# Attention backward: the crossbar transposes that TensorE still did, and GpSimd copies for dK, dV and dQ

## The chip, the cores and the metric

The kernel runs on one core of one Trainium2 chip. The core has five engines that each work through their own list of instructions in order: TensorE (PE in the profile, with its weight loads as PEld), VectorE (DVE), ScalarE (ACT), GpSimd (POOL) and SyncE (SP). SP computes nothing here; it issues DMAs, among them DMAs that transpose 128x128 blocks of two-byte elements on their way (DMA_TRANSPOSE, "the crossbar" below). POOL issues DMAs too. The metric is the device time of one execution in microseconds, as the median of several runs.

## The reference

The reference is one transformer block with adaptive layer norm, and the gradient of its output for nine of its inputs. With S = 2048 tokens, D = 512 and H = 32 heads of 16 columns each:

```
x = x + ga * (softmax(q k^T * 16**-0.5) v) wo        q, k, v = (layernorm(x)*(1+ca)+sa) wqkv
x = x + gb * (relu(h w1 + b1)**2 w2 + b2)            h = layernorm(x)*(1+cb)+sb
```

The change lies in the backward pass of the attention. For each head it forms again P = exp(scores), then dP = dO V^T (with the softmax correction folded into two extra columns), dS = P * dP, and from these

```
dV = P^T dO      dK = dS^T Q      dQ = dS K
```

dV and dK contract over queries, dQ over keys, so that dQ needs dS with its two axes turned.

## The kernel before, in words

The program has three stages: the forward pass with the weight gradients of the dense layer (to about 1166 us of the profiled span), the attention backward (`attn_bwd`, to about 2385 us), and a tail with the remaining weight gradients and the input gradient (`phase6`).

`attn_bwd` goes through 16 pairs of heads (g from 0 to 7, jp 0 or 1). A pair is worked off in 16 groups, numbered m: four chunks c of 512 keys, and in each the 16 blocks ib of 128 queries, four to a group. One query block against one chunk, for both heads, is a unit; i is its number in its group. For a unit

- TensorE makes the scores of each head (line 1608, `st`) and, a unit later, dP of each head (line 1522, `dp`); the two use different halves of the array's rows and run together;
- ACT takes the exponential (line 1611, `pu`);
- VectorE multiplies dS = dP * P (line 1526, `ds`). In ten of the 16 groups one of the eight products goes by ACT (a copy, line 1540) and POOL (line 1541) instead;
- TensorE adds to dK and dV of the chunk (line 1459, `acckv`). When all 16 query blocks of a chunk are in, ACT writes the sum to `kvT` (line 1462), still with features on partitions.

When a group's four units are done, `dS()` has SP issue one crossbar transpose of the group's 32 blocks of dS (line 1549, `dsT<-ds`; one of five destinations is a piece of a larger tile and is named `keep`). In the first group of each chunk TensorE turns four of the 32 blocks instead (line 1565, against an identity matrix), ACT copies them out of PSUM (line 1566), and SP's DMA takes 28. Below, T(m) is the crossbar transpose of group m.

dQ of two groups (`dq`, line 1484, `accq`) is put into TensorE's list two groups after the second of them was transposed: eight calls, two in each even unit. TensorE works in order: where `dsT` has not landed when such a matmul comes up, all that stands behind it waits as well, the next `st` and `dp` first.

When a pair is complete, its results have to be turned once more, tokens onto partitions. Both halves of `kvT` (8 blocks each) and `dqT` (4 blocks, written by VectorE on line 1492) go into a list `turnq`, and at the fourth unit of a group of the next pair (from group 2 on for `kvT`, from 7 on for `dqT`) one entry is taken: TensorE turns its blocks (lines 1472, 1500) into a PSUM buffer of the same three that `st` uses, and ACT copies them, spread over the heads' columns, into `dk_t`, `dv_t`, `dq_t` (lines 1476, 1502).

POOL meanwhile issues the loads for the next pairs (line 1597), about one for each group, each behind a copy of one element (`tick`, line 1596) that ties the load to the progress of VectorE.

The order on every engine in this stage is the order of the program; nothing is rearranged by a scheduler that matters here.

Of the kernel before, what the change touches and what calls it, by code (L numbers as in the profile page):

```python
# [9 lines left out]
BF16 = mybir.dt.bfloat16  # L10
# [9 lines left out]
P = 128  # L20
DH = 16
# [84 lines left out]
class K:  # L106
# [1284 lines left out]
    def load_group(self, g):  # L1391
# [5 lines left out]
        if g < 2:  # L1397
            T, o = {}, 0
            for n, e in width.items():
                if g:  # L1400
                    T[n] = qp.tile([P, e], BF16, name=f"{n}g")[:]
                elif n == "K":
                    T[n] = self.keep[:, :e]
                else:
                    T[n] = self.q0[:, o:o + e]
                    o += e
            self.Tq[g] = T
        T, pieces = self.Tq[g % 2], []
        for n, (src, rows) in fm.items():
# [21 lines left out]
    def attn_bwd(self):  # L1431
# [7 lines left out]
        tc, nc = self.tc, self.nc  # L1439
        S, D, H, NQ, ST, SC = self.S, self.D, self.H, self.NQ, self.ST, self.SC  # L1440
        G = 4
        W = 4 * DH
        kvp, stp, dpp = self.kvp, self.stp, self.dpp
# [3 lines left out]
        nc.vector.memset(acckv[:], 0.0)  # L1447
        accq = accp.tile([P, 512], F32, name="accq")
        masked, kvs = self.masked, self.kvs
        pend, pendq, turnq, two = [], [], [], []  # L1450
        own = dT_free[-1]

        def kv(u):
            (T, g, jp, c, ib, kvT, pu, ds) = u
            for j, (n, src) in enumerate((("Q", ds), ("dO", pu))):
                for a in range(2):
                    r = 64 * j + 32 * a
                    col = (2 * jp + a) * DH
                    nc.tensor.matmul(acckv[r:r + DH, :], lhsT=T[n][:, ib, col:col + DH], rhs=src[:, a, :],  # L1459
                                     start=(ib == 0), stop=(ib == ST - 1))  # L1460
            if ib == ST - 1:
                nc.scalar.activation(kvT[:, 512 * c:512 * (c + 1)], acckv[:], ACT.Copy, scale=kvs[:])

        def turn(g, jp, kvT, s0):

            if kvT is None:
                return turn_q(g, jp)
            h0 = 4 * g + 2 * jp
            n = ST // 2
            tp = stp.tile([P, n, P], BF16, name="st")  # L1470
            for st in range(n):
                nc.tensor.transpose(tp[:, st, :], kvT[:, (s0 + st) * P:(s0 + st + 1) * P], self.ident[:])
            v = tp[:].rearrange("p s (t a e) -> p t s a e", t=2, a=2)
            for t, dst in enumerate((self.dk_t, self.dv_t)):
                d = dst[:, s0:s0 + n, h0 * DH:(h0 + 2) * DH].rearrange("p s (a d) -> p s a d", a=2)
                nc.scalar.copy(d, v[:, t, :, :, 0:DH])

        def dq(u):
# [12 lines left out]
            if (c, ib0) == (SC - 1, ST - 2 * G):  # L1491
                nc.vector.tensor_scalar(self.dqT[:], accq[:], self.scale, None, ALU.mult)
                turnq.append((g, jp, None, 0))

        def turn_q(g, jp):

            h0 = 4 * g + 2 * jp
            tp = stp.tile([P, ST // G, P], BF16, name="st")
            for b in range(ST // G):
                nc.tensor.transpose(tp[:, b, :], self.dqT[:, b * P:(b + 1) * P], self.ident[:])  # L1500
            for h in range(2):
                nc.scalar.copy(self.dq_t[:, 8 * h:8 * h + 8, h0 * DH:(h0 + 2) * DH].rearrange("p (s i) e -> p s i e", i=2),
                               tp[:, 2 * h:2 * h + 2, :].rearrange("p i (s e) -> p s i e", s=G))

        def kv_two(n=2):
            for _ in range(n):
                u = pend.pop(0)
                kv(u)
                (T, g, jp, c, ib, kvT, pu, ds) = u
                if ib < ST - 1:  # L1510
                    continue
                if c % 2 and (g, jp) == (NQ - 1, 1):
                    turnq.append((g, jp, kvT, 4 * (c - 1)))
                elif c == SC - 1:
                    turnq.extend((g, jp, kvT, s0) for s0 in (0, ST // 2))

        def dP(u, a):

# [9 lines left out]
        def odd(c, ib):  # L1528
            return (c * SC + ib // G) % 2 == 1

        def no_turn(c, ib):
            return ib // G > 0

        def off(c, ib):
            return odd(c, ib) or (c > 1 and ib // G == 2)
# [1 line left out]
        def dP_pool(u, dp):  # L1537
            (T, g, jp, c, ib, kvT, pu, dsg, i, grp) = u
            f = (self.junk6, self.csq)[(c * SC + ib // G) % 2]
            nc.scalar.copy(f[:], dp[:])  # L1540
            nc.gpsimd.tensor_tensor(dsg[:, i, 1], f[:], pu[:, 1, :], ALU.mult)  # L1541
# [26 lines left out]
        tick = self.tick  # L1568
        wmt = self.load_wmt()
        T = self.T0  # L1570
        last = None
        for g in range(NQ):
            for jp in range(2):
                if jp == 0:
                    if g + 1 < NQ:
                        Tn, later = self.load_group(g + 1)
                    else:
                        Tn, later = None, self.wq_pieces(1) + wmt[2 * g + 1:]
                    cut = len(later) // 2 if Tn else len(later)
                    pieces = self.pair_pieces(g, 1) + wmt[2 * g:2 * g + 1] + later[:cut]  # L1580
                    later = wmt[2 * g + 1:2 * g + 2] + later[cut:]
                elif g + 1 < NQ:
                    pieces = self.pair_pieces(g + 1, 0) + later
                else:
                    pieces = [(self.xhat1_6[:, st, :], self.xhat1_d.rearrange("(st p) d -> p st d", p=P)[:, st, :])
                              for st in range(ST)]
                kvT = kvp.tile([P, S], BF16, name="kvT")
                end = (g, jp) == (NQ - 1, 1)
                total = len(pieces)
                for c in range(SC):  # L1590
                    c0 = 512 * c
                    for ib0 in range(0, ST, G):
                        m = c * (ST // G) + ib0 // G
                        while pieces and ((total - len(pieces)) * SC * ST <= m * G * total or m == SC * ST // G - 1):
                            if last:
                                nc.gpsimd.tensor_copy(tick[:], last[7][0:1, 0, 0, 0:1])
                            nc.gpsimd.dma_start(*pieces.pop(0))
                        dsg, grp = self.dsp.tile([P, G, 2, 512], BF16, name="ds"), []
                        for i in range(G):
                            ib = ib0 + i  # L1600
                            q = slice(ib * P, (ib + 1) * P)
                            if turnq and i == 3 and m >= (7 if turnq[0][2] is None else 2):
                                turn(*turnq.pop(0))
                            pu = self.pup.tile([P, 2, 512], BF16, name="pu")
                            for a in range(2):
                                stt = stp.tile([P, 512], F32, name="st")
                                rs = slice(64 * jp, 64 * jp + 64)
                                nc.tensor.matmul(stt[:], lhsT=T["QT"][rs, q], rhs=masked["KT"][a][rs, c0:c0 + 512],  # L1608
                                                 start=True, stop=True)
                                held = dP(last, a) if last else None  # L1610
                                nc.scalar.activation(pu[:, a, :], stt[:], ACT.Exp, scale=self.scale)  # L1611
                                if held is not None:
                                    dP_pool(last, held)
                                if a == 0 and i % 2 == 1 and odd(c, ib) and len(pend) >= 4:
                                    kv_two(1)
                            if last:
                                dS(last)
                            last = (T, g, jp, c, ib, kvT, pu, dsg, i, grp)
                            if i % 2 == 1 and len(pend) >= 4:
                                kv_two(1 if odd(c, ib) else 2)  # L1620
                            elif i % 2 == 0 and len(pendq) > 2 * G:
                                for _ in range(4 if end else 2):
                                    dq(pendq.pop(0))
                            if i == 2:
                                turn_ds(dsg, grp, no_turn(c, ib), end and m > 2)
            T = Tn
        with tc.manual_schedule(engines=ALL):
# [23 lines left out]
            self.cs_bc(2)  # L1651
            turn(*turnq.pop(0))
            self.dw_mm(k1, 1, 1, 0, ST)
        assert not turnq and not pend
        self.dw_open = [(1, 0, k0), (2, 0, v0), (1, 1, k1)]

    def dw_mm(self, pt, t, kt, a, b):
# [308 lines left out]
```

## Time and profile before

| what | value |
|---|---|
| median of 3 runs | 2506.41 us (2501.06 to 2510.86) |
| span of the profiled execution, first to last instruction | 2498.5 us |
| what the median has beyond that span (2506.41 - 2498.5) | 7.9 us |
| attention backward in that span | about 1166 to 2385 us |
| granted TensorE clock, mean | 0.998 |
| PE, ACT, DVE, POOL busy, share of the whole span | 96%, 91%, 68%, 30% |
| DMA_TRANSPOSE from `ds` in the stage | 256: 208 to `dsT`, 48 to `keep` |

No separate total time is given for the profiled execution; its span is set against the runs by the difference in the third row.

How to read it: shares over the whole span mix three stages, so each stage is read by its own stretch. A row of a group has the line, the engine, the operation, the tiles (out<-in) and the count, then busy time and the mean of one, then the engine's idle time just before these instructions, and what ended it. SP's DMA instructions are not counted as busy anywhere, but the timeline of the SP queue has a start and a duration for each, where the duration is the time that the instruction held the queue, not the time to landing. A row of the timeline with x4 covers four instructions, from the start of the first to the end of the last.

### The profile page before, as it was taken

The page shows a single profiled execution, that of the slowest core. Times are in us where ns is not written, and L with a number is a line of the kernel's source. Part 1 is how long each engine was busy: PE and PEld are TensorE (multiplying, and loading weights), DVE is VectorE, ACT ScalarE, POOL GpSimd, SP SyncE. Part 2 cuts the span into 40 slices and gives each one's busy share as a digit, 9 for nine tenths or more (in the row PEclk, how much of TensorE's full clock was granted, in tenths as well). Part 3 has the DMA queues.
Part 4 walks back from the last instruction along what each step waited for, and adds up shares of the span by engine and source line. Part 5 has one row for each costly group of instructions (what it writes and reads, how often), then busy time and mean ns, then how long its engine had stood idle before and what let it go on. Part 6 is the DMA issues. An engine that isn't in the chain of part 4 may idle for free.

```text
span 2498.5 us, 67897 instructions
## 1 busy us (share of the span) xinstructions
PE 2410.2 (96%) x26211; PEld 1061.6 (42%) x26439; DVE 1695.0 (68%) x3487; ACT 2283.1 (91%) x3757; POOL 753.5 (30%) x1337
## 2 busy tenths in 40 slices
PE   8999999999999999999999999999999999999998
PEld 4555555555555555583233332333333333333343
DVE  6222322422332343576999999999999999999957
ACT  7999999999999997534999999999999999999945
POOL 2344531220131022245222323322333222322223
PEclk9999999999999999999999999999999999999999
DMA  4589661541243045499999999999999999999997
GB/s 166 135 179 208 169 125 47 132 100 40 92 114 98 23 123 147 110 199 216 232 235 233 232 227 231 237 234 231 230 235 239 234 230 236 234 233 236 238 217 192
DMA packets 1293547, 454.13 MB, mean 182 GB/s; under 512 B 1236948, under 2 KB 1261398, under 8 KB 1293222
## 3 DMA queue, kind: packets, MB, share of 16 engines
q1 hardware_dynamic: 1252422, 344.68, 71.8%
q0 software_dynamic: 38720, 104.04, 13.9%
q8 instruction: 207, 3.39, 0.6%
q10 hardware_dynamic: 2080, 1.05, 0.2%
q14 instruction: 118, 0.97, 0.1%
HBM read 75.83 MB, written 64.49 MB: 56 GB/s over the span
## 4 chain that ended last, share of the span: by engine, by line
PE 49%; ACT 35%; DMA 7%; issue 5%; DVE 3%; POOL 1%; SPq 1%; ACTq 0%; DVEq 0%; POOLq 0%
ACT pu L391 26%; PE st L1608 17%; PE acckv L1459 8%; ACT pu L1611 6%; DMA dsT<-ds 5%; PE accq L1484 5%; PE st L388 4%; PE dp L1522 2%; PE accbank L322 2%; PE dps L1050 2%; PE dp L1659 1%; PE st L1754 1%; ACT csq L1540 1%; PE pps L1237 1%; DVE ds L1526 1%
## 5 line engine op out<-in xcount | busy, mean ns | idle before, releaser
L1526 DVE TENSOR_TENSOR ds<-dp,pu 128x512 bf16<-128x512 f32 x1888 | 1166.0, 682 | 34.6 <-PE dp L1522 19.1
L1611 ACT ACTIVATE pu<-st 128x512 bf16<-128x512 f32 x2048 | 1073.8, 666 | 34.7 <-PE st L1608 21.3
L391 ACT ACTIVATE pu<-st 128x1024 bf16<-128x1024 f32 x992 | 912.1, 1077 | 4.2 <-PE st L388 3.7
L388 PE MATMUL st<-QTm,KTq 128*128 128x512 bf16 x1859 | 560.9, 377 | 27.1 <-ACT pu L391 6.1
L322 PEld LDWEIGHTS <-pu 128*128 128x128 bf16 x8192 | 346.7, 96 | 236.1 <-issue 3.0
L1522 PE MATMUL dp<-kvm,q 64*128 64x512 bf16 x1024 | 365.0, 384 | 2.0 <-DVE ds L1526 0.7
L322 PE MATMUL accbank<-Vaug,pu 128*128 128x17 bf16 x8192 | 357.4, 171 | 8.3 <-ACT Vaug L522 1.1
L1522 PE MATMUL dp<-kvm,dOTg 64*128 64x512 bf16 x1024 | 363.6, 383 | 0.3
L1608 PE MATMUL st<-kvm,q 64*128 64x512 bf16 x1024 | 349.4, 382 | 5.4 <-ACT pu L1611 0.2
L1608 PE MATMUL st<-kvm,QTg 64*128 64x512 bf16 x1024 | 348.1, 381 | 6.5
L1541 POOL TENSOR_TENSOR ds<-csq,pu 128x512 bf16<-128x512 f32 x128 | 147.2, 1150 | 627.0 <-ACT csq L1540 553.6
L388 PEld LDWEIGHTS <-KTq 128*128 128x128 bf16 x1984 | 188.4, 96 | 176.9 <-issue 124.8
L1459 PE MATMUL acckv<-ds,Qg 128*16 128x512 bf16 x1024 | 176.2, 382 | 0.3
L1459 PE MATMUL acckv<-pu,q 128*16 128x512 bf16 x1024 | 176.3, 383 | 0.0
L1459 PE MATMUL acckv<-ds,q 128*16 128x512 bf16 x1024 | 176.2, 383 | 0.0
L1459 PE MATMUL acckv<-pu,dOg 128*16 128x512 bf16 x1024 | 176.0, 382 | 0.0
L302 POOL DMA_DIRECT2D QTm<-QTq_d x124 | 63.1, 511 | 341.5 <-PE st L388 320.0
L1608 PEld LDWEIGHTS <-q 64*128 64x128 bf16 x1024 | 67.0, 94 | 163.5 <-issue 150.6
L1608 PEld LDWEIGHTS <-QTg 64*128 64x128 bf16 x1024 | 67.1, 94 | 160.6 <-issue 145.7
L329 DVE RECIPROCAL rl<-accbank 128x4 f32<-128x4 f32 x128 | 22.9, 179 | 158.3 <-PE accbank L322 158.2
L1522 PEld LDWEIGHTS <-q 64*128 64x128 bf16 x1024 | 88.8, 93 | 52.9 <-issue 43.3
L1522 PEld LDWEIGHTS <-dOTg 64*128 64x128 bf16 x1024 | 88.2, 93 | 52.9 <-issue 43.8
(390 smaller groups left out, 3055.1 us busy)
## 6 DMA issues: line engine op xcount, KB each, us to landing
KTq<-KTq_d POOLq DMA_DIRECT2D x24, 512.0 KB, 3.9
duT_d<-auT POOLq DMA_DIRECT2D x3, 1792.0 KB, 7.9
aT_d<-rT POOLq DMA_DIRECT2D x3, 1792.0 KB, 11.5
KTq_d<-KTq SPq DMA_DIRECT2D x32, 128.0 KB, 2.1
QTq_d<-ev_fm SPq DMA_DIRECT2D x32, 128.0 KB, 4.3
ktm_d<-ev_tm POOLq DMA_DIRECT2D x32, 128.0 KB, 2.5
VTq_d<-vT POOLq DMA_DIRECT2D x4, 1024.0 KB, 6.3
dx<-dx_d SPq DMA_DIRECT2D x16, 256.0 KB, 4.6
```

The lines of the kernel that those rows point to most:

```text
L302: nc.gpsimd.dma_start(QTm[j][32 * j:32 * j + 32, :], self.QTq_d[g, 32 * j:32 * j + 32, 512 * qc:512 * (qc + 1)])
L322: nc.tensor.matmul(acc[:, a, sub, :], lhsT=pu[:, a, sub * P:(sub + 1) * P], rhs=Vaug[:, kb, h, :], start=(kb == 0 and a == 0 and sub == 0) ...
L388: nc.tensor.matmul(stt[:, a, :], lhsT=KT[:, kb * P:(kb + 1) * P], rhs=QTm[2 * jp + a][:], start=True, stop=True)
L391: nc.scalar.activation(pu[:], stt[:], ACT.Exp, scale=self.scale)
L1050: nc.tensor.matmul(pt[:], lhsT=a[st], rhs=g_tm[:, st, :], start=(st == 0), stop=(st == ST - 1))
L1459: nc.tensor.matmul(acckv[r:r + DH, :], lhsT=T[n][:, ib, col:col + DH], rhs=src[:, a, :], start=(ib == 0), stop=(ib == ST - 1))
L1484: nc.tensor.matmul(accq[r:r + 32, o:o + 256], lhsT=T["K"][:, 4 * c + sub, col:col + 32], rhs=v[:, r // 32 % 2 * 2:r // 32 % 2 * 2 + 2, 4 * ...
L1522: nc.tensor.matmul(dp[:], lhsT=T["dOT"][rd, ib * P:(ib + 1) * P], rhs=masked["VT"][a][rd, 512 * c:512 * (c + 1)], start=True, stop=True)
L1526: nc.vector.tensor_tensor(dsg[:, i, a], dp[:], pu[:, a, :], ALU.mult)
L1541: nc.gpsimd.tensor_tensor(dsg[:, i, 1], f[:], pu[:, 1, :], ALU.mult)
L1608: nc.tensor.matmul(stt[:], lhsT=T["QT"][rs, q], rhs=masked["KT"][a][rs, c0:c0 + 512], start=True, stop=True)
L1611: nc.scalar.activation(pu[:, a, :], stt[:], ACT.Exp, scale=self.scale)
```

## The change

After it, TensorE turns nothing in pairs 0 to 14 of the attention backward:

- `no_turn` is always true, so that all 32 blocks of every group go through the crossbar. The four TensorE transposes and the ACT copy in the first group of each chunk are gone, and 64 of the 256 transposes on SP grow from 28 to 32 blocks.
- A half of `kvT` goes into `turnq` as soon as its two chunks are complete, not at the pair's end; `kvT` is made once for all pairs.
- An entry of `turnq` is handed to the new `cross`, which issues a crossbar transpose on SP of 8 blocks (`kvT`) or 4 blocks (`dqT`) into an idle part of the tile `keep`, and gives back a function `spread`. Two groups later that function is called: two copies on POOL from there into `dk_t` and `dv_t`, or into the two halves of `dq_t`.
- In the last pair (`end`) entries are still turned by TensorE, as before.

```diff
-                if c % 2 and (g, jp) == (NQ - 1, 1):
+                if c % 2:
                     turnq.append((g, jp, kvT, 4 * (c - 1)))
-                elif c == SC - 1:
-                    turnq.extend((g, jp, kvT, s0) for s0 in (0, ST // 2))
...
         def no_turn(c, ib):
-            return ib // G > 0
+            return True
...
-                            if turnq and i == 3 and m >= (7 if turnq[0][2] is None else 2):
-                                turn(*turnq.pop(0))
+                            if spreads and i == 3 and m >= spreads[0][0]:
+                                spreads.pop(0)[1]()
+                            if turnq and i == 3 and m % 8 >= (7 if turnq[0][2] is None else 2):
+                                if end:
+                                    turn(*turnq.pop(0))
+                                else:
+                                    spreads.append((m + 2, cross(*turnq.pop(0))))
```

```diff
+        def cross(g, jp, kvT, s0):
+
+            h0 = 4 * g + 2 * jp
+            n = ST // 2
+            tk = self.keep[:, ST * P:(ST + n) * P].rearrange("p (s k) -> p s k", k=P)
+            tq = self.keep[:, (ST + n) * P:(ST + n + ST // G) * P].rearrange("p (s k) -> p s k", k=P)
+            if kvT is None:
+                nc.sync.dma_start_transpose(tq, self.dqT[:])
+
+                def spread():
+                    for h in range(2):
+                        nc.gpsimd.tensor_copy(
+                            self.dq_t[:, 8 * h:8 * h + 8, h0 * DH:(h0 + 2) * DH].rearrange("p (s i) e -> p s i e", i=2),
+                            tq[:, 2 * h:2 * h + 2, :].rearrange("p i (s e) -> p s i e", s=G))
+            else:
+                nc.sync.dma_start_transpose(tk, kvT[:, s0 * P:(s0 + n) * P])
+
+                def spread():
+                    v = tk.rearrange("p s (t a e) -> p t s a e", t=2, a=2)
+                    for t, dst in enumerate((self.dk_t, self.dv_t)):
+                        d = dst[:, s0:s0 + n, h0 * DH:(h0 + 2) * DH].rearrange("p s (a d) -> p s a d", a=2)
+                        nc.gpsimd.tensor_copy(d, v[:, t, :, :, 0:DH])
+            return spread
```

The order of SP's queue in the second pair, before: from T(12) of the first pair on, one transpose for each group (the third number is the shape, partitions x blocks x 128).

```order
L1549 DMA_TRANSPOSE dsT_19898<-ds 128x28x128
L1549 DMA_TRANSPOSE dsT_19899<-ds 128x32x128
L1549 DMA_TRANSPOSE dsT_19900<-ds 128x32x128
L1549 DMA_TRANSPOSE keep<-ds 128x32x128
L1549 DMA_TRANSPOSE dsT_19897<-ds 128x28x128
L1549 DMA_TRANSPOSE dsT_19898<-ds 128x32x128
L1549 DMA_TRANSPOSE dsT_19899<-ds 128x32x128
L1549 DMA_TRANSPOSE dsT_19900<-ds 128x32x128
```

The same queue after, around groups 2 to 10 of a pair: T(2) is the first row behind the first `kvT` row.

```order
L1510 DMA_TRANSPOSE keep<-kvT 128x8x128
L1571 DMA_TRANSPOSE keep<-ds 128x32x128
L1571 DMA_TRANSPOSE dsT_19897<-ds 128x32x128
L1571 DMA_TRANSPOSE dsT_19898<-ds 128x32x128
L1571 DMA_TRANSPOSE dsT_19899<-ds 128x32x128
L1571 DMA_TRANSPOSE dsT_19900<-ds 128x32x128
L1502 DMA_TRANSPOSE keep<-dqT 128x4x128
L1571 DMA_TRANSPOSE keep<-ds 128x32x128
L1571 DMA_TRANSPOSE dsT_19897<-ds 128x32x128
L1571 DMA_TRANSPOSE dsT_19898<-ds 128x32x128
L1510 DMA_TRANSPOSE keep<-kvT 128x8x128
L1571 DMA_TRANSPOSE dsT_19899<-ds 128x32x128
```

Every group has 32 blocks, and a pair has three more transposes: ahead of T(2), T(7) and T(10). Over all pairs the queue has 43 rows more, 29 for `kvT` and 14 for `dqT`.

ACT before, in groups 2 to 4 of a pair (`pu` is the exponential; x8 are eight in a row):

```order
L1476 COPY dk_t<-st 128x8x32
L1476 COPY dv_t<-st 128x8x32
L1611 ACTIVATE pu<-st 128x512 x8
L1540 COPY csq<-dp 128x512
L1476 COPY dk_t<-st 128x8x32
L1476 COPY dv_t<-st 128x8x32
L1611 ACTIVATE pu<-st 128x512 x8
L1566 COPY dsT_19897<-st 128x512
L1611 ACTIVATE pu<-st 128x512 x2
L1462 ACTIVATE kvT<-acckv,kvs 128x512
```

After, only the exponentials, the copies for POOL (`csq`, `junk`) and the `kvT` rows are left there. The copies to `dk_t`, `dv_t` and `dq_t` now stand on POOL; here they are after the cross in group 2 and the one in group 7:

```order
L1516 COPY dk_t<-keep 128x8x32
L1516 COPY dv_t<-keep 128x8x32
L1618 COPY tick<-ds 1x1
L1619 DMA WmT<-WmT_d 128x384
L1563 TENSOR_TENSOR ds<-csq,pu 128x512
```

```order
L1563 TENSOR_TENSOR ds<-csq,pu 128x512
L1506 COPY dq_t<-keep 128x8x32 x2
L1618 COPY tick<-ds 1x1
L1619 DMA Qg<-qtm_d 128x256
```

Each pair of copies comes between a product of `ds` and the next `tick` and load.

More of the change, by code (lines that the diff above doesn't have):

```diff
@@ L1449, in attn_bwd @@
         masked, kvs = self.masked, self.kvs
-        pend, pendq, turnq, two = [], [], [], []
+        pend, pendq, turnq, spreads, two = [], [], [], [], []
         own = dT_free[-1]
@@ L1570, in attn_bwd @@
         T = self.T0
+        kvT = kvp.tile([P, S], BF16, name="kvT")
         last = None
@@ L1586, in attn_bwd @@
                               for st in range(ST)]
-                kvT = kvp.tile([P, S], BF16, name="kvT")
                 end = (g, jp) == (NQ - 1, 1)
@@ L1653, in attn_bwd @@
             self.dw_mm(k1, 1, 1, 0, ST)
-        assert not turnq and not pend
+        assert not turnq and not pend and not spreads
         self.dw_open = [(1, 0, k0), (2, 0, v0), (1, 1, k1)]
```

## The prediction

> **What bounds the kernel now.** I read the page first, then the busy time of the attention backward alone (fourteen pairs of it), then SP's own queue. The stretch has PE, PEld, DVE, ACT and POOL busy, each with its count, then the granted clock, the DMA share and GB/s:
>
> ```profile
> 1254.00:2305.00 1051.00, 1036.98 (x11238) 324.21 (x11235) 1025.10 (x1662) 1041.92 (x2123) 312.28 (x600) 1.00 1.21 233
> L1526 DVE TENSOR_TENSOR ds<-dp,pu 128x512 bf16<-128x512 f32 x1888 | 1166.0, 682 | 34.6 <-PE dp L1522 19.1
> ```
>
> PE, ACT and DVE are all 97.5 to 99% busy in it, at full clock; POOL alone has room. VectorE's products, which the change does not touch, sit idle for only 34.6 us in the whole stage: whatever is taken from PE and ACT, not much more than that can come off the time. So the question is what the rest of the machine has left, and the answer is in SP's queue:
>
> ```profile
> L1549 SPq DMA_TRANSPOSE dsT<-ds x208: 3490/4262/6457, 1173.4 to 2377.8; - x104
> L1549 SPq DMA_TRANSPOSE keep<-ds x48: 3550/4204/5392, 1192.2 to 2300.7; - x48
> DMA to landing us min/median/max: 5.1/7.2/9.0
> ...
> 1477.28 3.93 SPq L1549 DMA_TRANSPOSE keep<-ds  x1
> 1481.32 20.41 SPq L1549 DMA_TRANSPOSE dsT<-ds  x4
> 1501.84 4.57 SPq L1549 DMA_TRANSPOSE keep<-ds  x1
> 1506.62 19.11 SPq L1549 DMA_TRANSPOSE dsT<-ds  x4
> 1525.83 4.11 SPq L1549 DMA_TRANSPOSE keep<-ds  x1
> 1530.04 19.53 SPq L1549 DMA_TRANSPOSE dsT<-ds  x4
> 1549.67 4.14 SPq L1549 DMA_TRANSPOSE keep<-ds  x1
> 1554.01 4.06 SPq L1549 DMA_TRANSPOSE dsT<-ds  x1
> ```
>
> A transpose holds the queue for a median of 4.26 us, and there are 256 in the 1208.7 us from 1173.4 to 2382.1 (2377.8 plus the last one's 4.3). Added up over the rows of the timeline (the first two rows here group them: 256) the durations come to 1119.8 us, 93% of that time. In the pair shown, the fifth, the queue has no pause at all: each row starts 0.10 us after the last one ended (1477.28 + 3.93 = 1481.21, next 1481.32), which is the handover. So 255 handovers take 25.5 us more, and the queue has 1208.7 - 1119.8 - 25.5 = 63.4 us left in the whole stage, 4 us a pair. A fourth resource is nearly full, and the page's busy table does not list it.
>
> What happens where it is full, the same pair shows on PE and DVE (the last bracket is the idle time before and its end):
>
> ```profile
> 1499.57 0.29 PE L1484 MATMUL accq<-dsT,keep 128*32 128x256 bf16 x2
> 1500.76 0.40 PE L1484 MATMUL accq<-dsT,keep 128*32 128x256 bf16 x6 [0.90 <-DMA dsT<-ds]
> ...
> 1488.06 0.68 DVE L1492 TENSOR_SCALAR dqT<-accq 128x512 bf16<-128x512 f32 x1
> 1501.72 6.67 DVE L1526 TENSOR_TENSOR ds<-dp,pu 128x512 bf16<-128x512 f32 x11 [1.15 <-PE dp L1522]
> 1540.01 25.14 DVE L1526 TENSOR_TENSOR ds<-dp,pu 128x512 bf16<-128x512 f32 x40 [1.00 <-PE dp L1522]
> 1565.07 0.68 DVE L1492 TENSOR_SCALAR dqT<-accq 128x512 bf16<-128x512 f32 x1
> 1640.77 0.68 DVE L1492 TENSOR_SCALAR dqT<-accq 128x512 bf16<-128x512 f32 x1
> ```
>
> A late `dsT` stops dQ on PE, and a moment later VectorE has no `dp`. `dqT` is written once a pair, so its rows are the pair's clock: 1565.07 - 1488.06 = 77.0 us with the full queue, 1640.77 - 1565.07 = 75.7 us for the next pair. Late transposes are rare so far:
>
> ```profile
> PE accq L1484 <- DMA dsT<-ds: 7.2, 11, 2.9
> ```
>
> That is 7.2 us in 11 waits over the stage; the queue is full, but mostly in time.
>
> **What the change removes.** The rows of the work that leaves PE and ACT, for the stage:
>
> ```profile
> L1566 ACT COPY dsT<-st 128x512 bf16<-128x512 bf16 x51 | 30.7, 603 | 0.3
> L1565 PE MATMUL st<-ident,ds 128*128 128x128 bf16 x252 | 25.0, 222 | 0.0
> L1472 PE MATMUL st<-ident,kvT 128*128 128x128 bf16 x256 | 19.8, 220 | 0.1
> L1476 ACT COPY dv_t<-st 128x256 bf16<-128x256 bf16 x32 | 12.8, 401 | 0.0
> L1476 ACT COPY dk_t<-st 128x256 bf16<-128x256 bf16 x32 | 12.5, 392 | 2.7 <-PE st L1472 2.3
> L1502 ACT COPY dq_t<-st 128x256 bf16<-128x256 bf16 x32 | 10.9, 410 | 0.0
> ```
>
> That is about 67 us on ACT and 45 us and a little on PE. Little of it is on the path. The run of 53 products (33.28 us, 0.63 each) that covers a turn of `ds`, with its copy at 1607.22, has no pause; where a half of `kvT` is turned, with the copy at 1635.80, VectorE does pause:
>
> ```profile
> 1607.22 0.62 ACT L1566 COPY dsT<-st 128x512 bf16<-128x512 bf16 x1
> 1635.80 0.37 ACT L1476 COPY dk_t<-st 128x256 bf16<-128x256 bf16 x1
> 1599.81 33.28 DVE L1526 TENSOR_TENSOR ds<-dp,pu 128x512 bf16<-128x512 f32 x53 [0.20 <-ACT pu L1611]
> 1633.76 2.48 DVE L1526 TENSOR_TENSOR ds<-dp,pu 128x512 bf16<-128x512 f32 x4 [0.66 <-PE dp L1522]
> 1636.57 4.28 DVE L1526 TENSOR_TENSOR ds<-dp,pu 128x512 bf16<-128x512 f32 x7 [0.33 <-ACT dv_t L1476]
> ```
>
> So removing the turns of `ds` is worth nothing: VectorE's products, eight in each of the groups where they stand, cover them, and if VectorE were faster they would cost up to their 30.7 us of ACT. The turns of `kvT` show 0.66 + 0.33 = 1.0 us of idle VectorE; over the 15 pairs whose results are turned inside the next pair, that is 15 us, and the ceiling is the 34.6 us above. If nothing else changed, the kernel would be 15 (0 to 35) us faster.
>
> **What it adds to SP's queue.** Blocks that TensorE turned are now issued by SP. Rows for small transposes, from the opening of the kernel (4 blocks, then 8 blocks):
>
> ```profile
> L646 SPq DMA_TRANSPOSE ev_tm<-KTq x32: 1190/1204/2621, 61.2 to 244.4; - x32
> L705 SPq DMA_TRANSPOSE vT<-vpad x16: 1232/1450/2318, 126.5 to 224.0; - x16
> ```
>
> Step by step:
> - 64 transposes grow by 4 blocks. 4.26 us / 32 = 0.133 us a block, so 64 x 0.53 = 34 us. By the minimum of the 28-block ones, 3.49 / 28 = 0.125, it is 32 us.
> - 29 transposes of 8 blocks. They cost more than their blocks (8 x 0.133 = 1.07): at least 1.23, median 1.45 us where other loads ran beside them. I take 1.31: the 1.23, raised as the 32-block ones are raised here over their own least (32 x 0.125 = 4.0, median 4.26). 29 x 1.31 = 38 us; the bounds are 36 (1.23) and 67 (2.32).
> - 14 transposes of 4 blocks at 1.19 raised the same way, 1.27: 17.8 us; the bounds are 16.7 and 36.7 (2.62).
> - 43 handovers of 0.10: 4.3 us.
>
> Together 94 us (89 to 142) into a queue that has 63.4 us left. The rest, 94 - 63.4 = 31 us (25 to 79), has nowhere to go but the end. In a pair: 70.0 us of issue today, plus 16 x 0.133, 2 x 1.31, 1.27 and 19 handovers of 0.10, is 77.9 us, against 75.7 us in the undisturbed pair above. The turned-off work on PE and ACT then buys nothing, because VectorE waits for `dp`, `dp` stands behind dQ, and dQ waits for `dsT`.
>
> I do not let the 4.26 us fall under load: in the full pair the queue never pauses, and its sixteen rows from 1477.28 to 1553.81 still average 4.8 us from start to start.
>
> [...]
>
> **What it adds to POOL and elsewhere.** 86 copies of 256 elements, for which the trace has no like; between the `tick` of one element and a two-input product twice the size:
>
> ```profile
> L1596 POOL COPY tick<-ds 1x1 bf16<-1x1 bf16 x257 | 45.4, 177 | 105.2 <-DVE ds L1526 105.2
> L1541 POOL TENSOR_TENSOR ds<-csq,pu 128x512 bf16<-128x512 f32 x127 | 146.1, 1150 | 620.8 <-ACT csq L1540 547.4 <-DVE ds L1526 73.4
> ```
>
> 0.18 to 1.15 us each, I take 0.5; six a pair, 3 us. POOL waits 620.8 us for its products' inputs in the stage, so I cost this at nothing; without that cover it would be 86 x 0.5 = 43 us. The new wait is POOL's for the landing of the cross. Behind it stand a load and, a group later, a product of `ds`. The cross is issued behind T(m-1), so at most a group (4.7 us) after its place in the program, and lands some 4 us later if it is as far ahead of the 7.2 us of the long ones as its issue is shorter (7.2 - 4.26 + 1.31 = 4.3). The copies come two groups (9.4 us) after its place, which leaves 0.4 us at the least. POOL may wait there a little once the queue is late. The queue's wait on ACT for `kvT` and on DVE for `dqT` costs nothing: both are written a group or more ahead.
>
> **The rivals.** *The crossbar keeps up* (the other side). If issue drops to its least, 4.0 us for 32 blocks and 1.2 for the small ones, a pair needs 16 x 4.0 + 2 x 1.23 + 1.19 + 1.9 = 69.6 us, below the 74.7 us (75.7 - 1.0) that PE, ACT and DVE would need. It decides from an average of 4.3 us for 32 blocks on, where the sum above has (70.0 + 2.1) / 16 = 4.5. For it: such durations occur, half of all being below 4.26. Against it: the average over a whole pair is nowhere near the least. Then the 15 us come through: 2506 - 15 = 2491 us. [...]
>
> *The added issue just fits*: part of today's durations is a wait behind the transpose before, which a steadier queue may lose. At 2% less each, 22 of the 31 us go and 9 are left: 2515 us, no change that can be told. For it: the 2% is well inside the spread of 3.49 to 6.46 us. Against it: the full pair above shows longer durations, not shorter.
>
> *POOL becomes the late one*: the landing of a cross, itself behind a backed-up queue, holds POOL for about 1 us in each of 43 places, and the product of `ds` behind it delays the transpose of its group. That comes on top: 2506 + 31 + 43 = 2580 us. Against it: POOL's 620.8 us of waiting.
>
> **How the numbers follow.** Chances: the queue sets the pace 0.60, keeps up 0.17, just fits 0.17, POOL 0.06. The likeliest gives a span of 2498.5 + 31 = 2529.5 us; with the 7.9 us by which the median of the runs shown lies above the profiled span, 2537 us. Its own range is 2520 (25 less 11, part of the 15 that compute gives back) to 2585 (79). For 8 in 10 I reach down over the no-change case to 2497 and stop at 2562, since the upper bounds of the small transposes come from a few disturbed ones. A change of 0.5%, 12.5 us, is about what a measurement of this kernel can tell from none. Faster by more has the 0.17 of its case; within 0.5% has 0.17 and 0.03 from the low end of the first case; slower has the rest, 0.63.
>
> **What would show it.** Right: SP's timeline shows rows that start 0.10 us after the last ended in nearly all pairs, the `dqT` rows stand 77 to 78 us apart, the wait of PE `accq` for `dsT` grows from 7.2 us to tens, and the idle time of `ds` behind PE `dp` grows by about as much; PE and ACT are less busy in the stage. The small transposes take 1.2 to 1.5 us. Wrong: pauses in SP's queue as today with `dqT` rows 74 to 75 us apart (it keeps up), a 32-block transpose that falls towards 4.0 us when the queue is full, or POOL idle behind `keep` (the third rival).

## The result, and the profile after

| | median | runs |
|---|---|---|
| before | 2503.73 us | 4, 2500.91 to 2510.86 |
| after | 2588.89 us | 4, 2581.57 to 2597.14 |

The change makes the kernel slower: the ratio is 1.0334, with a 95% interval of 1.0300 to 1.0367, some 85 us. The direction was forecast, the size was not: the forecast was 2537 us, +31, and the time lies outside the range of 2497 to 2562 us. The spans of the two profiled executions, 2498.5 and 2586.6 us, differ by 88 us, and nearly all of it is in the attention backward: from the first transpose of dS to the end of the last are 1210.3 us before and 1293.3 us after.

First three pieces of the page after: the engines' shares of the chain that ended last, the busiest groups of VectorE and ACT, and the queue of SP's transposes:

```profile
PE 40%; DMA 29%; ACT 19%; issue 5%; DVE 4%; SPq 2%; POOL 1%; DVEq 0%; POOLq 0%; ACTq 0%
...
L1548 DVE TENSOR_TENSOR ds<-dp,pu 128x512 bf16<-128x512 f32 x1888 | 1170.6, 682 | 113.7 <-PE dp L1544 72.6
L1638 ACT ACTIVATE pu<-st 128x512 bf16<-128x512 f32 x2048 | 1079.7, 613 | 123.9 <-PE dp L1544 87.6
...
q1 hardware_dynamic: 1323430, 362.51, 75.0%
```

VectorE's products take about as long as before, 1170.6 us against 1166.0 for the same 1888, but the idle time in front of them went from 34.6 to 113.7 us: +79, most of the loss. 72.6 us of it end with `dp` from TensorE, where it was 19.1. DMA is now 29% of the chain that ended last, and was 7%. The queue of SP's transposes (q1) moved 362.5 MB, and before, by the same row of its page, 344.68 MB in 1252422 packets.

The stretch of fourteen pairs shows the same (PE, PEld, DVE, ACT, POOL busy, clock, DMA share, GB/s):

```profile
1254.00:2380.00 1126.00, 1044.12 (x10702) 270.82 (x10700) 1026.40 (x1657) 1024.18 (x1978) 341.84 (x682) 0.98 1.25 232
```

PE was busy 98.7% of its stretch and is now 92.7%; DVE went from 97.5 to 91.2%, ACT from 99.1 to 91.0%. The DMA rate stayed: 233 and 232 GB/s.

The granted TensorE clock fell from 1.00 to 0.98 in this stretch: by the clock's records in the trace it was one half for 11 short spells of 3.4 or 6.8 us in the stage, and before for one. This explains little of the loss. Of the pairs 1 to 13 after (each from one `dqT` row to the next, as below), the seven in which no such spell begins take 80.1 us on average and all thirteen 80.7; the thirteen of before take 75.2. Whether the waits bring the lower clock or the other way round is not shown.

Then SP's queue, its transposes by line, and in one pair:

```profile
L1571 SPq DMA_TRANSPOSE dsT<-ds x208: 3902/4469/7747, 1173.7 to 2461.0; - x104
L1571 SPq DMA_TRANSPOSE keep<-ds x48: 3952/4509/7161, 1192.8 to 2380.3; - x48
...
DMA to landing us min/median/max: 5.8/7.8/9.4
...
L1510 SPq DMA_TRANSPOSE keep<-kvT x29: 1301/1302/2017, 1224.3 to 2354.2; - x29
...
L1502 SPq DMA_TRANSPOSE keep<-dqT x14: 1262/1264/1277, 1287.5 to 2338.2; - x14
...
1609.56 8.77 SPq L1571 DMA_TRANSPOSE dsT<-ds  x2
1618.43 5.77 SPq L1571 DMA_TRANSPOSE keep<-ds  x1
1624.25 1.30 SPq L1510 DMA_TRANSPOSE keep<-kvT  x1
1625.66 17.66 SPq L1571 DMA_TRANSPOSE dsT<-ds  x4
1643.42 4.23 SPq L1571 DMA_TRANSPOSE keep<-ds  x1
```

Each row starts about 0.1 us after the last one ended, as it did in the one full pair before. Added up over all rows of the timeline, the 256 transposes of dS take 1196.5 us (1119.8 before), the 43 new ones 57.0 us, and 298 handovers of 0.10 us 29.8 us. From the first start to the last end are 1293.3 us, so that 10 us of pauses are left. The same sum gives 65 for the kernel before (the prediction's 63.4 took the last transpose for one of average length). The queue is full for the whole stage, not for one pair.

What waits for it:

```profile
PE accq L1484 <- DMA dsT<-ds: 50.0, 55, 2.1
POOL dk_t L1516 <- DMA keep<-kvT: 40.4, 27, 3.9
...
PE accq L1484 <- DMA keep<-ds: 11.4, 11, 1.7
...
1584.62 0.68 DVE L1492 TENSOR_SCALAR dqT<-accq 128x512 bf16<-128x512 f32 x1
...
1587.98 4.88 DVE L1548 TENSOR_TENSOR ds<-dp,pu 128x512 bf16<-128x512 f32 x8 [0.30 <-PE dp L1544]
...
1663.55 0.68 DVE L1492 TENSOR_SCALAR dqT<-accq 128x512 bf16<-128x512 f32 x1
```

TensorE waits 61.4 us for turned dS (50.0 + 11.4), where it waited 7.2, or 8.5 with the last groups of the stage. The pair shown takes 78.9 us (1663.55 - 1584.62) where an undisturbed one took 75.7; it is one of the shorter ones, which go from 78.2 to 82.4 in the pairs 1 to 13. POOL waits for the landing of `kvT` in 27 of 29 places.

### The profile page after: what moved, and what is told of

It is laid out like the page before. It is cut to its first block, busy times and chain, and to the rows that moved or that the text cites. A ratio compares the mean times of both kernels' runs of the same rounds, so it can differ in the third digit from the quotient of the medians.

```text
span 2586.6 us, 67011 instructions
## 1 busy us (share of the span) xinstructions
PE 2438.3 (94%) x25895; PEld 1005.0 (39%) x25895; DVE 1697.8 (66%) x3487; ACT 2265.0 (88%) x3607; POOL 784.3 (30%) x1423
## 3 DMA queue, kind: packets, MB, share of 16 engines
q1 hardware_dynamic: 1323430, 362.51, 75.0%
q0 software_dynamic: 38720, 104.04, 14.1%
q10 hardware_dynamic: 2080, 1.05, 0.1%
## 4 chain that ended last, share of the span: by engine, by line
PE 40%; DMA 29%; ACT 19%; issue 5%; DVE 4%; SPq 2%; POOL 1%; DVEq 0%; POOLq 0%; ACTq 0%
DMA dsT<-ds 20%; ACT pu L391 17%; PE st L1635 9%; PE st L388 8%; DMA keep<-ds 6%; PE acckv L1459 4%; PE accq L1484 3%; PE accbank L322 3%; DVE ds L1548 2%; PE dps L1050 2%; PE dp L1544 2%; PE pps L1237 1%; SPq L1764 1%; PE pps L631 1%; PE pps L1255 1%
## 5 line engine op out<-in xcount | busy, mean ns | idle before, releaser
L1548 DVE TENSOR_TENSOR ds<-dp,pu 128x512 bf16<-128x512 f32 x1888 | 1170.6, 682 | 113.7 <-PE dp L1544 72.6
L388 PE MATMUL st<-QTm,KTq 128*128 128x512 bf16 x1984 | 587.9, 377 | 19.7 <-ACT pu L391 6.0
L1544 PE MATMUL dp<-kvm,dOTg 64*128 64x512 bf16 x1024 | 369.6, 388 | 14.4 <-DVE ds L1548 13.5
L1635 PE MATMUL st<-kvm,QTg 64*128 64x512 bf16 x1024 | 338.4, 389 | 0.6
L1635 PE MATMUL st<-kvm,q 64*128 64x512 bf16 x1024 | 336.1, 387 | 0.3 <-ACT pu L1638 0.2
L1484 PE MATMUL accq<-dsT,keep 128*32 128x256 bf16 x1632 | 112.1, 280 | 24.9 <-DMA dsT<-ds 24.3
L1635 PEld LDWEIGHTS <-q 64*128 64x128 bf16 x1024 | 67.2, 94 | 173.2 <-issue 171.8
L1484 PE MATMUL accq<-dsT,Kg 128*32 128x256 bf16 x1696 | 109.6, 282 | 25.8 <-DMA dsT<-ds 25.8
```

The source lines that it names most:

```text
L388: nc.tensor.matmul(stt[:, a, :], lhsT=KT[:, kb * P:(kb + 1) * P], rhs=QTm[2 * jp + a][:], start=True, stop=True)
L1484: nc.tensor.matmul(accq[r:r + 32, o:o + 256], lhsT=T["K"][:, 4 * c + sub, col:col + 32], rhs=v[:, r // 32 % 2 * 2:r // 32 % 2 * 2 + 2, 4 * ...
L1544: nc.tensor.matmul(dp[:], lhsT=T["dOT"][rd, ib * P:(ib + 1) * P], rhs=masked["VT"][a][rd, 512 * c:512 * (c + 1)], start=True, stop=True)
L1548: nc.vector.tensor_tensor(dsg[:, i, a], dp[:], pu[:, a, :], ALU.mult)
```

## The experiments

Three theories stood at the start. **U** is the prediction's: SP's queue had some 63 us of pauses that could be used, and what goes beyond them costs. **Q**: the crossbar was fully used already before the change, so every block costs. **P**: POOL's waits for the crosses hold up its loads and products. A fourth, **K**, was formed on the way.

### One part alone: dS

```diff
         def no_turn(c, ib):
-            return ib // G > 0
+            return True
```

> The kernel before, with one part of the change: all 32 blocks of dS of every group go through the crossbar; kvT and dqT are still turned by TensorE. Theory Q (the crossbar was fully used already before the change; the pauses in SP's queue were not spare): time goes with the blocks. 256 more on 7936 is 3.2% of the 1210 us of the stage, +39 us, ratio about 1.015. Theory U (the prediction's: 63 us of SP's queue could be used, only what goes beyond costs): +34 us of issue fit into 63 us, ratio 0.998 to 1.002. Theory P (POOL's wait for the landing of the crosses holds its loads and products up): no cross here, ratio 1.000.

Measured: 2539.41 us, before 2510.59 on the same chip, ratio 1.0121 (1.0082 to 1.0159). U and P fall for this part, which has no cross at all; Q's 1.015 lies in the interval. SP's rows in it:

```profile
L1549 SPq DMA_TRANSPOSE dsT<-ds x208: 3907/4450/8777, 1173.8 to 2411.6; - x104
L1549 SPq DMA_TRANSPOSE keep<-ds x48: 4035/4344/6109, 1193.5 to 2334.2; - x48
```

Summed up over the timeline they take 1200.7 us, 81 us more than before. The blocks explain 34 of that (64 x 0.53 us); the other 47 us are transposes of the same size that hold the queue longer. Pauses fell from 65 to 20 us, so 45 us of pauses were indeed used, but about as much (47 us) came back as longer durations.

### One part alone: kvT and dqT

The changed kernel with dS as before:

```diff
         def no_turn(c, ib):
-            return True
+            return ib // G > 0
```

> The other part alone: kvT and dqT through the crossbar with the copies on POOL, while TensorE still turns 4 of 32 blocks of dS in the first group of a chunk. Theory Q: 288 more blocks (29 x 8 + 14 x 4) are 3.6%, +44 us, ratio about 1.018, up to 1.024 by their longer issue (61 us). Theory U: 61 us of issue just fit into 63 us, and 15 us come back from PE and ACT: ratio 0.994 to 1.000. Theory P: nearly all of the loss is here, ratio about 1.03.

Measured: 2556.64 us, ratio 1.0176 (1.0137 to 1.0216), as Q has it. The two parts, 1.2 and 1.8%, add up to 3.0%, about the whole. For P this run would have to carry nearly all of the loss, and it carries a little over half.

### POOL's copies later

```diff
-                                    spreads.append((m + 2, cross(*turnq.pop(0))))
+                                    spreads.append((m + 4, cross(*turnq.pop(0))))
```

> The changed kernel, with the copies on POOL four groups after the cross in place of two, so that POOL does not wait for the landing. Theory P: the 40.4 us that POOL waits in the profile of the changed kernel go, and with them 20 to 60 us of the 85: ratio to before 1.010 to 1.025. Theories Q and U: POOL is not on the path, ratio 1.030 to 1.036 as for the changed kernel.

Measured: 2590.75 us, ratio 1.0314 (1.0277 to 1.0350), the changed kernel's. The copies wait for nothing now (their rows of the line's view; no idle time of POOL before them is listed):

```profile
L1516 POOL COPY dk_t<-keep x29: 389/401/409, 1242.5 to 2373.4; 128x256 bf16<-128x256 bf16 x29
L1516 POOL COPY dv_t<-keep x29: 386/398/400, 1242.9 to 2373.7; 128x256 bf16<-128x256 bf16 x29
```

The 40.4 us of POOL's waits are gone and the time is not: P falls, and POOL's waits cost nothing, as the prediction had it. The copies themselves stand in every run that has crosses, so that they cost nothing is not shown by this run alone; `e4_after_24` below has them too and is faster than before.

### Room on the crossbar, after and before

In both kernels every transpose of dS is cut to the last 24 of its 32 blocks (a line not shown here sets the destinations to zero once):

```diff
                 dsT, n = grp
+                n = max(n, 8)
```

> The changed kernel with a quarter less on the crossbar: each transpose of dS carries 24 of the 32 blocks, the first query block of each group is left out of dQ (its place is set to zero once), so dQ and what follows from it are wrong. All else, the crosses and POOL's copies too, is as in the change. It shows what the change gains on PE and ACT where the crossbar has room. Theories Q and U: 15 us less than before, 0 to 35, ratio 0.986 to 1.000, most likely 0.994. Theory P: POOL still waits for the crosses, ratio above 1.01.

> The kernel before with 24 of 32 blocks in every crossbar transpose of dS (where TensorE turns four, the crossbar takes the last 24); the blocks left out are zero, so dQ and what follows from it are wrong. It tells what the crossbar cost before. Theory Q (fully used already before): the time falls about as far as in e4_after_24, ratio 0.988 to 0.994. Theory U (only the waits for dsT that the profile shows, 7.2 us): ratio 0.996 to 0.999. The difference to e4_after_24 (0.9908) is what TensorE's and ACT's turns cost where the crossbar has room.

Measured: after with 24 blocks 2488.31 us, ratio to before 0.9908 (0.9873 to 0.9942); before with 24 blocks 2499.98 us, 0.9963 (0.9950 to 0.9977). The first rules out P, which had it above 1.01. The second is U's number, not Q's: with 342 us of pauses in its queue, the kernel before gains only about 9 us, so that is what it loses to the crossbar. The idle time of VectorE's products, first in the changed kernel with 24 blocks, then in the one before with 24:

```profile
L1548 DVE TENSOR_TENSOR ds<-dp,pu 128x512 bf16<-128x512 f32 x1888 | 1159.1, 683 | 14.9 <-PE dp L1544 5.0
```

```profile
L1526 DVE TENSOR_TENSOR ds<-dp,pu 128x512 bf16<-128x512 f32 x1888 | 1165.4, 684 | 23.3 <-PE dp L1522 8.8
```

Where the crossbar has room, taking the turns off TensorE and ACT is worth 0.55% (0.9963 - 0.9908), 14 us; the two intervals together leave 5 to 23 us. The change cannot collect it.

### The loads

POOL's loads for the groups of heads 2 to 7 are left out, so those pairs compute with older data; here for the changed kernel, later for the one before:

```diff
+        if g >= 2:
+            pieces = []
         return {n: t if n in fm else t.rearrange("p (st w) -> p st w", st=ST) for n, t in T.items()}, pieces
...
         pieces = []
+        if g >= 2:
+            return pieces
         for n, src, sh, rows in (("KT", self.KTq_d, 0, DH), ("VT", self.VTq_d, 2, DH + 2)):
```

> The changed kernel without POOL's loads (and their one-element copies) for the groups of heads 2 to 7: those pairs compute with the data of groups 0 and 1, so the gradients of the attention are wrong, and the work on all engines stays. It tells how much of a transpose's duration comes from the loads beside it. If the loads stretch it (4.67 us on average against 3.9 at the least): 0.25 to 0.5 us fall off each of about 220, 55 to 110 us, ratio to before 0.99 to 1.012. If the stretch comes from the transposes before it in the queue or from other traffic: ratio 1.025 to 1.034.

Measured: 2526.53 us, ratio 1.0068 (1.0041 to 1.0094), in the range for loads that stretch the transposes. Against the changed kernel's 1.0334 that is 2.7% less, some 67 us, with about 11 us either way by the two intervals; the profiled executions differ by 58 us (2586.6 and 2529.0). SP's queue is still full (17 us of pauses), but its transposes are shorter:

```profile
L1575 SPq DMA_TRANSPOSE dsT<-ds x208: 3910/4266/6096, 1175.2 to 2406.1; - x104
L1575 SPq DMA_TRANSPOSE keep<-ds x48: 3917/4270/5572, 1194.3 to 2326.6; - x48
```

Their sum is 1134.2 us against 1196.5, 62 us less, and nearly all of it is gone from the span (58 us). So here, with the queue full, what the loads took from the crossbar came straight out of the time.

### Less on the crossbar, and the order alone

The kernel before with four more blocks of dS on TensorE in group 6 of a pair:

```diff
         def no_turn(c, ib):
-            return ib // G > 0
+            return ib // G > 0 and (c, ib // G) != (1, 2)
```

> The kernel before, with four blocks of dS turned by TensorE in one more group of each pair (the third of the second chunk, group 6), so the crossbar has 4 blocks less a pair, 64 in all. Theory Q: 0.8% of the stage's crossbar time, up to 10 us less, ratio 0.996 to 0.999. Theory U: nothing on the crossbar side, and PE and ACT have 0.3 and 0.6 us more in a group that VectorE sets: ratio 1.000 to 1.004.

Measured: 2506.61 us, ratio 0.9994 (0.9971 to 1.0018), no change that can be told; the interval holds both theories' numbers.

The changed kernel's order with all turns done as before (`no_turn` as in `e2_cross_only`, and):

```diff
-                                if end:
+                                if True:
                                     turn(*turnq.pop(0))
```

> The changed kernel with the new places in the order (a half of kvT as soon as it is complete, in groups 10 and 2), but everything turned as before: kvT and dqT by TensorE with ACT's copies, and four blocks of dS in the first group of a chunk. It is the change's order without its crossbar and POOL work. All theories: one turn moves from group 3 to group 10, both lighter groups: ratio 0.997 to 1.003. If it is above 1.01, the loss of e2_cross_only is one of order and not of the crossbar.

Measured: 2511.48 us, ratio 1.0002 (0.9980 to 1.0024). The new places in the order cost nothing that can be told. So the loss of `e2_cross_only` is not one of order: it comes with the crosses and the copies on POOL that belong to them.

### Half the dose, and the loads before

By now Q was wrong about the kernel before and U about every addition. Theory K takes from both: before, the crossbar and the engines end together, so less on the crossbar gains little and more costs in full. Half of the first part alone tests it:

```diff
         def no_turn(c, ib):
-            return ib // G > 0
+            return ib // G > 0 or c < 2
```

> The kernel before, with all 32 blocks of dS on the crossbar in the first two of a pair's four chunks only (in the other two TensorE still turns four in the first group): 128 blocks more in all, half of e1_ds_only. Theory K (the kernel before stands just at the point where the crossbar takes over, and no part of its pauses is spare): half of what e1_ds_only lost, 1.2% / 2, ratio 1.004 to 1.008. Theory U (the pauses can be used, only the excess costs): 17 us fit into 63 us, ratio 0.998 to 1.001.

> The kernel before without POOL's loads for the groups of heads 2 to 7 (computes with old data there, gradients of the attention wrong; as e6_after_no_loads). Without them the crossbar has some 60 us more. Theory K: the kernel before is set by PE, ACT and VectorE too, so it gains only the waits for dsT, as with 24 blocks: ratio 0.993 to 0.998. If the crossbar alone set it: ratio about 0.975.

Measured: 1.0057 (1.0036 to 1.0078) for half the blocks, very near half of 1.21%; and 0.9943 (0.9924 to 0.9962) for the kernel before without the loads, 14 us less, where some 60 us fell off the changed kernel. K's ranges hold both. The wait of TensorE in the latter (`accq` for `dsT`):

```profile
PE accq L1488 <- DMA dsT<-ds: 8.2, 3, 5.3
```

That is 3 waits where the kernel before has 13 in the same window (1180 to 2400 us), but one is 5.3 us long, and the sum, 8.2 against 8.5 us, did not fall. So K's size is right here, but that the 14 us are these waits, as its expectation had it, is not shown.

The doses together, each worked out from the rows of SP's timeline (dS on average for 256; pauses are what is left after 0.10 us for each handover):

| kernel | blocks against before | mean of a dS transpose | pauses | ratio |
|---|---|---|---|---|
| before, no loads | 0 | 4.17 us | 114 us | 0.9943 |
| before, more on TensorE | -64 | 4.33 | 80 | 0.9994 |
| the change's order alone | 0 | 4.37 | 78 | 1.0002 |
| before | 0 | 4.37 | 65 | 1 |
| half of dS | +128 | 4.56 | 36 | 1.0057 |
| all of dS | +256 | 4.69 | 20 | 1.0121 |
| crosses only | +288 | 4.48 | 26 | 1.0176 |
| after, no loads | +544 | 4.43 | 17 | 1.0068 |
| after | +544 | 4.67 | 10 | 1.0334 |

All of dS has 4 blocks more in a quarter of its transposes, worth 0.13 us in this mean; from 4.37 to 4.69 are 0.32 us. The order alone moves the pauses by 13 us with the same blocks, so differences of that size in the pauses say nothing.

In bytes the additions are alike. A block is 128 x 128 x 2 bytes, 32 KB, and the total DMA rate between 1254 and 2300 us is 231 to 234 GB/s in every kernel of the table but the one before without loads (223). At the 233 GB/s of the kernel before, the bytes added by half of dS, all of dS, the crosses and the whole change come to 18, 36, 41 and 77 us, an estimate. The ratios give 14, 30, 44 and 84 us, and each estimate lies within its interval. So what was added cost about the time of its bytes at the rate that the DMAs had already reached before, pauses in the queue or not. The other way it does not hold, as K has it: 64 blocks fewer are 9 us by the same estimate and gained nothing that can be told. Whether the limit lies in the crossbar, in the DMA engines or in something that both use, no run tells apart.

## Why the prediction was right and wrong

**What bounds the kernel** was read rightly: SP's queue as the fourth nearly full resource, the late `dsT` that stops dQ on TensorE, and VectorE idle behind `dp`. All three signs came: `accq` grew from 7.2 to 61.4 us, VectorE's idle time by 79 us, and the queue has 10 us of pauses left in 1293.3. Only the pair's clock missed its sign: 77 to 78 us were forecast, 78.2 to 82.4 came.

**What the change removes** was right: nothing for the turns of dS that VectorE covers, 15 us in all; the two kernels with 24 blocks differ by 14 us (5 to 23). They do not separate the two kinds of turns, so that the dS turns are worth nothing is still only argued.

**The prices of the new transposes** were right: 1.31 and 1.27 us forecast, medians 1.302 and 1.264 us measured; 38 + 17.8 us forecast for all, 57.0 us measured. In part that is luck: the prediction raised the least duration of such rows by the stretch of the long ones, but these hardly stretch (the least are 1.301 and 1.262 us). The prediction's estimate of the least for 32 blocks, 4.0 us (32 x 0.125), lies near what was measured: in the changed kernel, where all 256 transposes of dS have 32 blocks, none took less than 3.90 us. In that kernel's full queue they took 4.67 us on average, and 4.67 us for 1.05 MB are 225 GB/s.

**The step that failed** is the one worded "I do not let the 4.26 us fall under load". They did not fall; they rose, and the prediction had no term for that. It took today's durations (1119.8 us) plus 34 us for the blocks, 1153.9 us in all, and found 63.4 us left in the queue. Measured are 1196.5 us: 42.6 us more, 0.17 us for each of the 256. The pauses were used nearly as forecast, 55 us of them, but in the same measure the transposes became longer, so they paid for little; the loss by bytes above fits this too, since the DMAs were at 233 GB/s already while the queue paused. In numbers: 57.0 for the crosses, 76.7 for dS (34 and 42.6) and 4.3 for handovers are 138 us, less 55 us of pauses, +83 us in the queue; the forecast was 94 less 63.4.

The rise was to be seen before. The full pair that the prediction itself quoted, sixteen transposes in 76.7 us, had 4.8 us from start to start, and the sum per pair still used the average of all pairs, 1119.8 / 256 = 4.37 us. With the full pair's rate, 4.8 x 16 = 76.8 us plus 0.53 x 4 for the blocks, 1.31 x 2 + 1.27 and 3 handovers give 83.1 us a pair, where 81.0 us were measured (mean distance of the ends of dS of the middle pairs): too much by 2 us, where the forecast's 77.9 was too little by 3. A duration measured beside pauses was used as the price of an instruction in a queue without any.

**The rivals**: "keeps up" and "just fits" fall by the result. "POOL becomes the late one" was right that POOL would wait (40.4 us), and wrong on its price: in `e3_spread_late` the waits are gone and the time stays. Its 2580 us lies close to the 2589 measured by luck. So does the upper end of the likeliest case's own range, 2585 us: it came from small transposes of 2.32 and 2.62 us, and they took 1.30 and 1.26.

**Open** is why a transpose holds the queue longer in the kernels whose queue has fewer pauses (4.37 us with 65 us of them, 4.67 with 10). That it waits for room behind the transposes ahead of it fits the landing times (median 7.2 us before, 7.8 after), but no run shows it apart. The loads are one part of the long durations: without them the mean falls by 0.21 us before (4.37 to 4.17) and by 0.24 us after (4.67 to 4.43). With the queue full and most loads gone it is still 0.5 us above the least.

The experiments do not point to a version that beats both: the only faster ones leave work out, one more turn on TensorE gains nothing, and to collect the 9 us that the crossbar costs the kernel before, somebody would have to take blocks from it.

## What to carry to other kernels

A queue that does not appear among the engines' busy times can be the fourth resource in a balanced kernel, as SP's was here (10 us of pauses in 1293.3 us); add up the durations on it before moving work there. Its pauses need not be spare time: take the price of an instruction from a stretch in which the queue is full, since the durations beside pauses were too short here (4.37 us on average before, 4.67 after), and look whether the bytes per second already stand still (233 and 232 GB/s here). When several engines are equally full, removing work from some of them by loading another can be a loss, as it was here (ratio 1.0334), even where the work removed is real (14 us): the end went with the one that was loaded.

## What the runs showed of the hardware that was not expected

- The total DMA rate in this stage was 233 GB/s before and 232 after (the rows of the two long stretches), with the crossbar's bytes up by 17.8 MB (362.51 - 344.68). The stage grew with its bytes, although the queue that issues them went from 65 us of pauses to 10.
- POOL's loads cost a full crossbar queue 58 to 67 us (by the spans and by the ratios) for 13 MB (104.04 - 91.05 MB on POOL's own DMA queue, the second number from the page without loads), and one with pauses 14 us (0.57%).
- A transpose of 4 blocks holds the queue nearly as long as one of 8, 1.264 and 1.302 us in the median, where 32 blocks take 4.47.
- In the records of single packets, the crossbar's queue moved less than 100 GB/s for a microsecond or more 103 times in the changed kernel without loads; 93 of these stretches begin within 1.5 us of a packet on the queue that the page lists as `instruction` (q8), of which there is one about every 13 us, so that chance alone would give about 24. In the trace of the changed kernel itself, counted in steps of 0.1 us, it is 89 of 98. It is a coincidence in time: no run changed it, and what the one has to do with the other is not shown.
